# GateLoop and SwiGLU: one masked product per head and chunk, with complex gate products per 256 steps, in place of seven levels of products

## The chip, the cores and the metric

The kernel runs on one NeuronCore of a Trainium2 chip. The metric is the device time of one execution in microseconds (us). Engines are named as the profile names them: PE is TensorE (PEld its weight loads), DVE is VectorE, ACT is ScalarE, POOL is GpSimd, SP is SyncE, which here only issues DMAs. Everything is float32, except that three weight matrices arrive as float64.

## The reference, cut to what matters

Batch 4, 8 heads, 768 steps, 48 features in a head; then a SwiGLU feed-forward on 3072 tokens of width 384 with a hidden width of 1536.

```python
mag = np.sqrt(a_re * a_re + a_im * a_im)
scale = np.minimum(mag, 0.999) / (mag + 1e-06)
a_re_n, a_im_n = (a_re * scale, a_im * scale)
for t in range(S):
    new_re = ar * S_re - ai * S_im          # ar, ai: gates of step t, one per feature of k
    new_im = ar * S_im + ai * S_re
    kv = np.einsum('bhd,bhe->bhde', k[:, :, t], v[:, :, t])
    S_re, S_im = (new_re + kv, new_im)
    y[:, :, t] = np.einsum('bhd,bhde->bhe', q[:, :, t], S_re)
...
rms = np.sqrt(np.mean(x * x, axis=-1, keepdims=True) + 1e-06)
xn = x / rms * rms_g
g = xn @ w_gate
silu = g * (1.0 / (1.0 + np.exp(-g)))
val = xn @ w_val
return (silu * val @ w_out).astype(np.float32)
```

The gates of the test data have magnitudes from 0.850 to 1.045.

## The kernel before, in words

The work is cut into 24 chunks of 128 steps (six in each batch). The lines below are those of the profile.

**Gates** (`gates`, L89 to L162). For each batch and each of three slabs of 128 rows (head, feature) one pass over [128 x 768] turns the gates into a unit phasor and a magnitude (L103 to L126, with one `reciprocal` at L111), then multiplies up the phasors since the sequence's first step: a tree of complex products on strided views (`cmul`, L130, six instructions each; recorded at L98, where the helper `tt` stands). Cosine, sine and magnitude go to DRAM and come back by chunk with (head) on the free axis (L268 to L272).

**Levels** (`levels`, L278 to L337). Rotated q and k ([96 x 1024]: 96 rows of cosine and sine parts, 8 heads of 128 steps) meet in products for the diagonal (`s_diag`, L295), and then for each level m = 1, 2, 4, 8, 16 (`s_low`, L310, 64 instructions of 16 moving columns for a chunk and level) and m = 32, 64 (`s_high`, L322). After each level DVE masks the product into `dg` (L313) and multiplies half of q and half of k by the gates' products of the halves (L327, L328; recorded at L282), which the next level's products wait for. The result is the matrix of weights `amat`.

**Finish** (`finish`, L339 to L388). k is transposed (`kt_ps`, L350), the state's increment is a product with v (`state_ps`, L354), the output of a chunk has steps on the partitions (`y_ps`, L366 from `amat`, L368 from the state); it is normalised (L372 to L378, with a power on POOL at L376), transposed by PE (`xT_ps`, L385) and scaled (L386).

**Feed-forward** (`feed_forward`, L391 to L416) for groups of three chunks: `gate_ps` and `val_ps` (L400, [128 x 384], 36 products each), a sigmoid on ACT (L403), two products on DVE (L404, L405), then `out_ps` (L410) and the store (L415). A float32 product shows as two MATMUL instructions and two weight loads. **Weights** of 8 bytes are made float32 by DVE (`narrow`, L229 to L250), 18 pieces of [128 x 768], nine instructions each.

**Order.** The program is written out as one sequence: all gates of batch 0 come first (L418 to L425), then `step` (L431) turns between a chunk's levels, the finish of the chunk before, the gates of the next batch and, as a filler, the weights or the feed-forward. The order that runs on each engine is the framework's: a planner goes through the sequence with its own costs and gives each engine the earliest instruction of the sequence that its costs make ready, as far as buffers (the `bufs` of a tile's tag) are free. So the conversion of weights runs between the gates' instructions of batch 0, though it stands behind them in the sequence. On each engine and queue the resulting order is fixed: whoever waits holds up everything behind it. All DMAs are issued from the SP queue.

Of the kernel before, what the change touches and what calls it, by code (L numbers as in the profile page):

```python
# [12 lines left out]
"""  # L13
# [16 lines left out]
P = 128  # L30
C = 128          # steps in a chunk
BLK = 32         # steps in a diagonal block
# [3 lines left out]
SCALE = 2.0 ** 30    # gates are scaled by a power of two before they are squared  # L36
TINY = 2.0 ** -112   # squares of scaled gates below this: the gate's own value is 0 in float32
# [3 lines left out]
def gateloop_swiglu(  # L41
    ctx: ExitStack,
    tc: tile.TileContext,
    qT: bass.AP,      # [B * NCH, D, H * C]
    kT: bass.AP,      # [B * NCH, D, H * C]
    v: bass.AP,       # [B * S, H * D]
    a_re: bass.AP,    # [B, H * D, S]
    a_im: bass.AP,    # [B, H * D, S]
# [4 lines left out]
    out: bass.AP,     # [B * S, H * D]  # L53
# [7 lines left out]
    N = B * NCH  # L61
# [142 lines left out]
    def load_weights(stage):  # L204
# [299 lines left out]
```

## Time and profile before

| | us |
|---|---|
| median of 3 runs | 1413.6 |
| lowest, highest | 1412.28, 1414.24 |
| span of the profiled execution, first to last instruction | 1409.9 |
| first matmul starts at | 214.36 |
| PE, DVE, ACT busy in the span | 997.1, 1072.7, 225.6 |
| mean granted TensorE clock, share of 2.4 GHz | 0.896 |

The profiled execution is one of its own, and its span is the sum's measure; the median of the three timed runs lies 3.7 us above it, which is taken for what lies around the span. The page also cuts the span into 40 slices of 35 us: PE shows 0 in the first six, 4 to 9 tenths afterwards, and DVE 7 to 9 tenths up to slice 33.

### The profile page before, as it was taken

Reading aid. Unit: us, or ns where it says so; the run is one execution under the profiler, and the core shown is the slowest. Engines: PE = TensorE matmul, PEld = TensorE weight load, DVE = VectorE, ACT = ScalarE, POOL = GpSimd, SP = SyncE. Lnnn points to the kernel's source line nnn. Section 1 sums busy time; section 2 is a strip of 40 time slices with the busy share of each in tenths; the row PEclk is TensorE's granted clock in tenths of the full one; section 3 lists DMA queues with packets and bytes.
Section 4 is the critical chain, followed back from the end, with each engine's and each line's share of the span. In section 5 each row is a group of like instructions: output and inputs, shape, how many; then the busy total and the mean of one; then the engine's idle time right before and its main releaser. Section 6 shows DMA issues by size and latency. Waiting matters only on the chain.

```text
span 1409.9 us, 30973 instructions
## 1 busy us (share of the span) xinstructions
PE 997.1 (71%) x13352; PEld 702.6 (50%) x13352; DVE 1072.7 (76%) x2663; ACT 225.6 (16%) x453; POOL 34.1 (2%) x54
## 2 busy tenths in 40 slices
PE   0000005245399869986999699869997999799898
PEld 0000005235266555655665666556656667666555
DVE  7999998998988978897899798978955642543120
ACT  1000001111032211211222113112111211111110
POOL 2000000000100000000000000000000000000000
PEclk9999999999999958995899599958995997699899
DMA  6223242241022222302222313021213021100000
GB/s 173 69 99 106 84 119 63 74 136 45 24 75 62 85 62 53 97 29 52 74 57 85 82 39 96 31 73 30 63 63 80 24 52 40 30 1 7 12 1 17
DMA packets 63993, 86.94 MB, mean 62 GB/s; under 512 B 5488, under 2 KB 48496, under 8 KB 63856
## 3 DMA queue, kind: packets, MB, share of 16 engines
q1 hardware_dynamic: 63856, 84.96, 21.5%
q8 instruction: 105, 1.72, 0.5%
q14 instruction: 32, 0.26, 0.1%
HBM read 66.06 MB, written 18.87 MB: 60 GB/s over the span
## 4 chain that ended last, share of the span: by engine, by line
PE 51%; DVE 39%; issue 6%; ACT 1%; DMA 1%; POOL 1%; SPq 0%; POOLq 0%; DVEq 0%; ACTq 0%
PE gate_ps L400 13%; PE val_ps L400 11%; PE out_ps L410 6%; PE s_high L322 5%; DVE k L282 4%; PE s_low L310 4%; PE y_ps L366 4%; DVE w L98 3%; DVE cs L282 3%; PE state_ps L354 3%; PE y_ps L368 3%; DVE re L98 3%; DVE mg L111 2%; DVE s L98 2%; DVE m L98 2%
## 5 line engine op out<-in xcount | busy, mean ns | idle before, releaser
L400 PE MATMUL gate_ps<-xT,wg 128*128 128x384 f32 x576 | 231.7, 539 | 0.7 <-DVE xT L386 0.7
L400 PE MATMUL val_ps<-xT,wv 128*128 128x384 f32 x576 | 205.2, 492 | 0.0
L410 PE MATMUL out_ps<-wo,hT 128*128 128x384 f32 x576 | 192.0, 490 | 0.0
L295 PE MATMUL s_diag<-q,k 96*32 96x32 f32 x1536 | 23.4, 228 | 218.2 <-DVE k L282 214.4
L310 PE MATMUL s_low<-cs,k 96*32 96x16 f32 x7680 | 111.0, 199 | 86.0 <-DVE k L282 77.0
L310 PEld LDWEIGHTS s_low<-cs,k 96*32 96x32 f32 x7680 | 97.8, 131 | 131.2 <-issue 65.8
L400 PEld LDWEIGHTS val_ps<-xT,wv 128*128 128x128 f32 x576 | 110.9, 194 | 79.7 <-issue 5.7
L400 PEld LDWEIGHTS gate_ps<-xT,wg 128*128 128x128 f32 x576 | 113.1, 209 | 64.5 <-issue 13.8
L410 PEld LDWEIGHTS out_ps<-wo,hT 128*128 128x128 f32 x576 | 107.7, 190 | 71.3
L282 DVE TENSOR_TENSOR cs<-cs,bp 96x512 f32<-96x512 f32 x144 | 98.6, 685 | 49.9 <-PE s_high L322 49.7
L295 PEld LDWEIGHTS s_diag<-q,k 96*32 96x32 f32 x1536 | 20.4, 140 | 223.5 <-DVE k L282 214.4
L322 PE MATMUL s_high<-cs,k 96*32 96x32 f32 (+1 forms) x1152 | 79.2, 237 | 68.8 <-DVE k L282 47.4
L322 PEld LDWEIGHTS s_high<-cs,k 96*32 96x32 f32 (+1 forms) x1152 | 70.1, 150 | 88.7 <-issue 70.0
L404 DVE TENSOR_TENSOR sg<-gate_ps,sg 128x384 f32<-128x384 f32 x96 | 52.8, 550 | 63.7 <-ACT sg L403 63.4
L282 DVE TENSOR_TENSOR k<-k,bp 96x512 f32<-96x512 f32 x144 | 97.8, 679 | 0.0
L403 ACT ACTIVATE sg<-gate_ps 128x384 f32<-128x384 f32 x96 | 47.0, 489 | 276.2 <-PE gate_ps L400 263.0
L366 PE MATMUL y_ps<-v,amat 128*128 128x48 f32 x384 | 89.2, 334 | 0.7 <-ACT amat L324 0.7
L368 PE MATMUL y_ps<-state,cs 96*128 96x48 f32 x320 | 80.0, 340 | 0.0
L366 PEld LDWEIGHTS y_ps<-v,amat 128*128 128x128 f32 x384 | 75.2, 249 | 2.4 <-ACT amat L324 0.8
L405 DVE TENSOR_TENSOR hT<-val_ps,sg 128x384 f32<-128x384 f32 x96 | 53.1, 553 | 29.7 <-PE val_ps L400 29.6
L313 DVE COPY_PREDICATED dg<-pairs,s_low 128x128 f32<-128x128 int32 x120 | 41.3, 344 | 43.6 <-PE s_low L310 41.9
L368 PEld LDWEIGHTS y_ps<-state,cs 96*128 96x128 f32 x320 | 66.8, 258 | 0.0
(82 smaller groups left out, 1316.1 us busy)
## 6 DMA issues: line engine op xcount, KB each, us to landing
q<-in_q_dram SPq DMA_DIRECT2D x48, 192.0 KB, 3.4
k<-in_k_dram SPq DMA_DIRECT2D x48, 192.0 KB, 3.6
mg<-mag SPq DMA_DIRECT2D x48, 192.0 KB, 4.1
re<-in_a_re_dram SPq DMA_DIRECT2D x12, 384.0 KB, 3.2
im<-in_a_im_dram SPq DMA_DIRECT2D x12, 384.0 KB, 4.0
v<-in_v_dram SPq DMA_DIRECT2D x24, 192.0 KB, 2.6
raw<-in_w_gate_dram SPq DMA_DIRECT2D x6, 768.0 KB, 4.8
mag<-mg SPq DMA_DIRECT2D x12, 384.0 KB, 2.5
```

The source lines that it names most:

```text
L98: nc.vector.tensor_tensor(out=o, in0=x, in1=y, op=op)
L282: tt = lambda o, x, y: nc.vector.tensor_tensor(out=o, in0=x, in1=y, op=ALU.mult)
L295: nc.tensor.matmul(ps[bs, h], lhsT=k[:, h, bs], rhs=q[:, h, bs], start=True, stop=True)
L310: nc.tensor.matmul(ps[bs, h].rearrange("s (j r) -> s j r", r=m), lhsT=k[:, h, bs], rhs=rhs, start=True, stop=True)
L322: nc.tensor.matmul(ps[lo, h], lhsT=k[:, h, lo], rhs=qd[:, h, hi], start=True, stop=True)
L366: nc.tensor.matmul(ps[:, h], lhsT=am[:, h], rhs=vv[:, h], start=True, stop=prev is None)
L368: nc.tensor.matmul(ps[:, h], lhsT=qd[:, h], rhs=prev[:, h], start=False, stop=True)
L400: nc.tensor.matmul(p_, lhsT=w_[:, d, fs], rhs=xT[:, d], start=d == 0, stop=d == ND - 1)
L403: nc.scalar.activation(out=sg, in_=gp, func=AF.Sigmoid)
L404: nc.vector.tensor_tensor(out=sg, in0=gp, in1=sg, op=ALU.mult)
L405: nc.vector.tensor_tensor(out=hT[:, f], in0=vp, in1=sg, op=ALU.mult)
L410: nc.tensor.matmul(ps, lhsT=hT[:, f, i * C:(i + 1) * C], rhs=wo[:, f], start=f == 0, stop=f == NF - 1)
```

## The change

Features stay on the partitions and the work goes by 12 groups of 256 steps. Instead of unit phasors and levels it uses the complex products of the gates themselves since the group's first step, A, and the product R of the gates' inverse squared magnitudes: q is multiplied by A, and k by A times R, so that one product of q and k for a head and chunk, with a triangular mask, holds all weights (`chunk`). The state is turned by the group's whole product at a group's end (`turned`, through a small DRAM transpose and a swap of the halves by DMA). q and k are first copied DRAM to DRAM into row order (`rows_in`), multiplied with features on the partitions, written to DRAM and read back by chunk, for one group: 786 KB for each of `qd` and `kd` out, and four reads of 196 KB for each back. Reciprocal and square root are replaced by logarithm, exponential and a Newton step on ACT and DVE. y comes out with features on the partitions in slots of 64 rows, so that no transpose is needed before the feed-forward; the mean square over features is a product with ones (`rms`). The feed-forward takes 256 columns (two hidden tiles in one PSUM bank) and uses one Silu in place of a sigmoid and a product. Weights come by POOL's queue. At the end the ranges of R and of the sums are checked on the device; if they are exceeded, `step_by_step` (a loop over the steps, not shown) computes everything again.

```diff
--- before.py
+++ after.py
...
-    GC = 3               # chunks in a group of the feed-forward
+GC = 2
+T = GC * C
+L = 8
...
+    prep = work.enter_context(tc.tile_pool(name="prep", bufs=1))
+    unit = work.enter_context(tc.tile_pool(name="unit", bufs=2))
+    act = work.enter_context(tc.tile_pool(name="act", bufs=1))
+    ffn = work.enter_context(tc.tile_pool(name="ffn", bufs=2))
+    ps_f = work.enter_context(tc.tile_pool(name="ps_f", bufs=4, space=PSUM))
+    ps_s = work.enter_context(tc.tile_pool(name="ps_s", bufs=2, space=PSUM))
+    ps_m = work.enter_context(tc.tile_pool(name="ps_m", bufs=2, space=PSUM))
...
+    def sc_ln(o, x, **kw):
+        table = nc.scalar.preload_act_table_set("natural_log_exp_and_others")
+        behind(table, last_silu[0])
+        behind(sc(o, x, AF.Ln, **kw), table)
...
+        if slots:
+            for p0, r in slot_rows(ap[:, a:b]):
+                nc.gpsimd.dma_start(out=raw[p0:p0 + r.shape[0]], in_=r)
+        else:
+            nc.gpsimd.dma_start(out=raw, in_=ap.rearrange("(c p) f -> p c f", p=P)[:, c0:c1, a:b])
...
+        sc(tf, hi.bitcast(FP32), AF.Abs)
+        sc(hi.bitcast(FP32), hi.bitcast(FP32), AF.Sign)
+        ts(tf, tf, 1.125 * 2.0 ** -15, ALU.max)
+        ts(t, t, 3, ALU.logical_shift_left, 0x40000000, ALU.bitwise_xor)
+        ts(u, t, -2 ** 23, ALU.bitwise_and)
+        stt(uf, lo.bitcast(U32), 2.0 ** -52, uf, MUL, MUL)
+        tt(tf, tf, uf, ADD)
+        ts(t, t, 0x7FFFFFFF, ALU.bitwise_and)
+        tt(part, tf.rearrange("p (c f) -> p c f", f=cols), hi.bitcast(FP32).rearrange("p (c f) -> p c f", f=cols))
...
+    def norm(g):
+        u = G[g]
+        a3 = u["a3"] = prep.tile([P, L, 3, N], FP32, tag="a3", name="a3")
+        for i, x in ((1, "re"), (2, "im")):
+            nc.scalar.copy(out=blocked(a3[:, :, i]), in_=by_block(u[x]))
+        xa = prep.tile([P, 2, L, N], FP32, tag="xa", name="sq")
+        xb = prep.tile([P, 2, L, N], FP32, tag="xb", name="rs")
+        w, sq, rs, h = xa[:, 0], xa[:, 1], xb[:, 0], xb[:, 1]
+        sc(w, a3[:, :, 1], AF.Square)
+        sc(sq, a3[:, :, 2], AF.Square)
+        tt(w, w, sq, ADD)
+        sc_ln(h, w, bias=small)
+        sc(rs, h, AF.Exp, scale=-0.5)
+        sc(sq, rs, AF.Square)
+        tt(sq, sq, w)
+        sc(h, sq, AF.Identity, scale=-0.5, bias=c15, accum_out=guard[:, g:g + 1])
+        tt(rs, rs, h)
+        sc(h, rs, AF.Identity, scale=-EPS_MAG, bias=one)
+        ts(w, rs, CAP, MUL, 1.0, ALU.min)
+        tt(w, w, h)
+        a = a3[:, :, 1:3]
+        tt(a, a, w.unsqueeze(2).to_broadcast([P, L, 2, N]))
+        sc(a3[:, :, 0], a3[:, :, 2], AF.Copy, scale=-1.0)
+        sc(sq, rs, AF.Identity, scale=EPS_MAG, bias=one)
+        stt(sq, rs, 1.0 / CAP, sq, ALU.max, MUL)
+        r = h.rearrange("p i n -> p (i n)").rearrange("p (j t) -> p j t", j=ND)
+        sc(by_block(r), blocked(sq), AF.Square, accum_out=guard_sum[:, g:g + 1])
+        R = u["R"] = prep.tile([P, ND, T], FP32, tag="R", name="R")
+        for j in range(ND):
+            nc.vector.tensor_tensor_scan(out=R[:, j], data0=r[:, j], data1=r_max.to_broadcast([P, T]), initial=1.0,
+                                         op0=MUL, op1=ALU.min)
+        nc.scalar.copy(out=guard[:, NG * 2 + g * ND:NG * 2 + (g + 1) * ND], in_=R[:, :, T - 1])
...
+    def load_qk(g):
+        u = G[g]
+        for name, other in (("q", "re"), ("k", "im")):
+            pool, tag = (late[0], name) if late[0] else (prep, other)
+            u[name] = pool.tile([P, ND, T], FP32, tag=tag, name=name)
+            nc.sync.dma_start(out=u[name], in_=u[name, "rows"].rearrange("(j p) t -> p j t", p=P))
...
+    def products(g):
...
+        def cmul(x, y, m):
+            p, q = ta[:, 0, :, 0:m], tb[:, 0, :, 0:m]
+            tt(p, x[:, 1:2].to_broadcast([P, 2, m]), y[:, 1:3])
+            tt(q, x[:, 2:3].to_broadcast([P, 2, m]), y[:, 0:2])
+            tt(y[:, 1:3], p, q, ADD)
+        for i in range(1, L):
+            cmul(a3[:, i - 1], a3[:, i], N)
+        E = prep.tile([P, 3, N], FP32, tag="E", name="E")
+        nc.vector.tensor_copy(out=E[:, 1:3], in_=a3[:, L - 1, 1:3])
+        s = ND
+        while s < N:
+            ts(E[:, 0], E[:, 2], -1.0, MUL)
+            cmul(E[:, :, 0:N - s], E[:, :, s:N], N - s)
+            s *= 2
+        ts(E[:, 0], E[:, 2], -1.0, MUL)
+        m = N - ND
+        x, y = a3[:, 0:L - 1, :, ND:N], E[:, :, 0:m]
+        p, q = ta[:, :, :, 0:m], tb[:, :, :, 0:m]
+        shape = [P, L - 1, 2, m]
+        tt(p, x[:, :, 1:2].to_broadcast(shape), y[:, 1:3].unsqueeze(1).to_broadcast(shape))
+        tt(q, x[:, :, 2:3].to_broadcast(shape), y[:, 0:2].unsqueeze(1).to_broadcast(shape))
+        tt(x[:, :, 1:3], p, q, ADD)
+        nc.scalar.copy(out=a3[:, L - 1, 1:3], in_=E[:, 1:3])
+        A = prep.tile([P, 2, ND, T], FP32, tag="A", name="A")
+        for i in range(2):
+            nc.scalar.copy(out=by_block(A[:, i]), in_=blocked(a3[:, :, 1 + i]))
...
+        q, k, R = u["q"], u["k"], u["R"]
+        both = [P, 2, ND, T]
+        tt(k, k, R)
+        pool, tag = (late[0], "qa") if late[0] else (prep, "a3")
+        qa = pool.tile([P, 2, ND, T], FP32, tag=tag, name="qa")
+        tt(qa, A, q.unsqueeze(1).to_broadcast(both))
+        tt(A, A, k.unsqueeze(1).to_broadcast(both))
+        for name, t in (("kd", A), ("qd", qa)):
+            to = dram.tile([2, DM, T], FP32, tag=name, name=name + "_rows")
+            nc.sync.dma_start(out=to.rearrange("i (j p) t -> p i j t", p=P), in_=t)
+            for c in range(GC):
+                u[name, c] = unit.tile([D2, H, C], FP32, tag=name, name=name, bufs=3)
+                for i in range(2):
+                    nc.sync.dma_start(out=u[name, c][i * D:(i + 1) * D],
+                                      in_=to[i].rearrange("(h d) t -> d h t", d=D)[:, :, c * C:(c + 1) * C])
...
+    def chunk(g, c, state):
...
+        am = []
+        for a in range(2):
+            ps = ps_s.tile([C, hh, C], FP32, tag="s", name="s_ps")
+            for h in range(hh):
+                nc.tensor.matmul(ps[:, h], lhsT=k[:, a * hh + h], rhs=q[:, a * hh + h], start=True, stop=True)
+            t = unit.tile([C, hh, C], FP32, tag="am", name="am", bufs=3)
+            tt(t, ps, mask.unsqueeze(1).to_broadcast([C, hh, C]))
+            am.append(t)
...
+            ps = ps_m.tile([D2, H, D], FP32, tag="m", name="z_ps")
+            for h in range(H):
+                nc.tensor.matmul(ps[:, h], lhsT=kt[h // hh][:, h % hh], rhs=vv[:, h, 0:D], start=True, stop=True)
+            new = states[count[0] % 2]
+            count[0] += 1
+            if state is None:
+                nc.vector.tensor_copy(out=new[:, :, 0:D], in_=ps)
+            else:
+                tt(new[:, :, 0:D], state[:, :, 0:D], ps, ADD)
+        ps = ps_m.tile([P, NP, C], FP32, tag="m", name="y_ps")
+        for h in range(H):
+            to = ps[h % 2 * SLOT:(h % 2 + 1) * SLOT, h // 2]
+            nc.tensor.matmul(to, lhsT=vv[:, h], rhs=am[h // hh][:, h % hh], start=True, stop=state is None)
+            if state is not None:
+                nc.tensor.matmul(to, lhsT=state[:, h], rhs=q[:, h], start=False, stop=True)
+        x, s2 = u["x"], u["s2"]
+        cs = slice(c * C, (c + 1) * C)
+        sq = act.tile([P, NP, C], FP32, tag="ysq", name="ysq")
+        nc.scalar.copy(out=x[:, :, cs], in_=ps)
+        sc(sq, ps, AF.Square)
+        tt(sq[:, 0:2], sq[:, 0:2], sq[:, 2:4], ADD)
+        tt(s2[:, cs], sq[:, 0], sq[:, 1], ADD)
...
+        sc(w, ps, AF.Identity, scale=1.0 / DM, bias=eps)
+        sc_ln(h, w)
+        sc(rs, h, AF.Exp, scale=-0.5)
+        sc(h, rs, AF.Square)
+        tt(w, w, h)
+        sc(h, w, AF.Identity, scale=-0.5, bias=c15, accum_out=guard[:, NG + g:NG + g + 1])
+        tt(rs, rs, h)
+        for j in range(ND):
+            stt(x[:, j], x[:, j], gcol[:, j:j + 1], rs, MUL, MUL)
...
+    def hidden(g, f):
...
+        gp = ps_f.tile([P, FP, T], FP32, tag="f", name="gate_ps")
+        vp = ps_f.tile([P, FP, T], FP32, tag="f", name="val_ps")
+        for p_, w_ in ((gp, wg), (vp, wv)):
+            for i in range(FP):
+                fs = slice((f + i) * P, (f + i + 1) * P)
+                for d in range(ND):
+                    nc.tensor.matmul(p_[:, i], lhsT=w_[:, d, fs], rhs=x[:, d], start=d == 0, stop=d == ND - 1)
+        sg = ffn.tile([P, FP, T], FP32, tag="sg", name="sg")
+        last_silu[0] = sc(sg, gp, AF.Silu)
+        t = u["h", f] = ffn.tile([P, FP, T], FP32, tag="h", name="h", bufs=12)
+        tt(t, vp, sg)
...
+    load_gates(0)
+    rows_in(0)
+    load_qk(0)
+    norm(0)
+    products(0)
+    weights_in()
+    rows_in(1)
+    load_gates(1)
+    load_qk(1)
+    norm(1)
+    recurrence(0)
+    rms(0)
+    products(1)
+    rows_in(2)
+    load_gates(2)
+    load_qk(2)
+    norm(2)
+    recurrence(1)
+    rms(1)
+    for f in range(0, NF, FP):
+        weights_hidden(f)
+        for g in range(2):
+            hidden(g, f)
+    rows_in(3)
+    load_gates(3)
+    products(2)
+    for f in range(0, NF, FP):
+        weights(wo, w_out, False, f, f + FP, 0, DM)
+    early.close()
+    late[0] = work.enter_context(tc.tile_pool(name="late", bufs=1))
+    load_qk(3)
+    recurrence(2)
+    rms(2)
+    norm(3)
+    rows_in(4)
+    load_gates(4)
+    for g in range(2):
+        outputs(g)
+    products(3)
+    load_qk(4)
+    norm(4)
+    for g in range(2, NG):
+        if g + 3 < NG:
+            rows_in(g + 3)
+            load_gates(g + 3)
+        if g + 1 < NG:
+            recurrence(g + 1)
+        for f in range(0, NF, FP):
+            hidden(g, f)
+        if g + 2 < NG:
+            products(g + 2)
+        if g + 3 < NG:
+            load_qk(g + 3)
+        if g + 1 < NG:
+            rms(g + 1)
+        if g + 3 < NG:
+            norm(g + 3)
+        outputs(g)
+    work.close()
...
+    ts(ok[:, 0:NG], guard_sum, SUM_MAX, ALU.is_le)
+    ts(ok[:, NG:], guard, R_MAX, ALU.is_lt)
+    nc.vector.tensor_reduce(out=good, in_=ok, axis=mybir.AxisListType.X, op=ALU.min)
+    bad = fin.tile([1, 1], I32, name="bad")
+    with tc.tile_pool(name="ps_c", bufs=1, space=PSUM) as ps_c:
+        ps = ps_c.tile([1, 1], FP32, name="good_ps")
+        nc.tensor.matmul(ps, lhsT=good, rhs=one, start=True, stop=True)
+        ts(bad, ps, P - 0.5, ALU.is_lt)
+    taken = nc.values_load(bad[0:1, 0:1], min_val=0, max_val=1)
+    with tc.If(taken > 0):
+        step_by_step(tc, qT, kT, v, a_re, a_im, out, H, wg, wv, wo, gcol, ident)
...
```

## Rows read from the trace of the kernel before

**Rows 1.** The page's part 1, busy time of each engine over the span.
```profile
PE 997.1 (71%) x13352; PEld 702.6 (50%) x13352; DVE 1072.7 (76%) x2663; ACT 225.6 (16%) x453; POOL 34.1 (2%) x54
```
**Rows 2.** Busy time by stretch: length, busy per engine, granted clock, DMA share, GB/s.
```profile
0.00:211.00 211.00, 0.00 (x0) 0.00 (x0) 203.13 (x508) 12.36 (x14) 9.54 (x30) 1.00 0.37 108
...
500.00:700.00 200.00, 164.68 (x2353) 118.23 (x2353) 169.26 (x431) 40.80 (x80) 4.37 (x5) 0.77 0.23 61
...
1100.00:1200.00 100.00, 97.87 (x1240) 66.70 (x1238) 45.92 (x88) 15.84 (x36) 0.67 (x2) 0.92 0.14 36
```
**Rows 3.** Waits: who waited for whom, total us, times, longest.
```profile
PE s_diag L295 <- DVE k L282: 214.4, 1, 214.4
```
**Rows 4.** The page's part 4, engines' shares of the chain that ended last.
```profile
PE 51%; DVE 39%; issue 6%; ACT 1%; DMA 1%; POOL 1%; SPq 0%; POOLq 0%; DVEq 0%; ACTq 0%
```
**Rows 5.** Groups on VectorE by line: count | busy us, mean ns | idle before.
```profile
L282 DVE TENSOR_TENSOR cs<-cs,bp 96x512 f32<-96x512 f32 x144 | 98.6, 685 | 49.9 <-PE s_high L322 49.7
L282 DVE TENSOR_TENSOR k<-k,bp 96x512 f32<-96x512 f32 x144 | 97.8, 679 | 0.0
...
L111 DVE RECIPROCAL mg<-mg 128x768 f32<-128x768 f32 x12 | 59.3, 4943 | 0.0
L98 DVE TENSOR_TENSOR w<-im 128x192 f32<-128x192 f32 (+6 forms) x216 | 59.1, 274 | 0.0
...
L405 DVE TENSOR_TENSOR hT<-val_ps,sg 128x384 f32<-128x384 f32 x96 | 53.1, 553 | 29.7 <-PE val_ps L400 29.6
...
L282 DVE TENSOR_TENSOR k<-k,cs 96x1024 f32<-96x1024 f32 x24 | 29.1, 1213 | 0.3 <-issue 0.3
```
**Rows 6.** Timeline of VectorE in the first stage: start us, us, instruction.
```profile
21.94 0.95 DVE L98 TENSOR_TENSOR w<-w,r 128x768 f32<-128x768 f32 x1
22.81 0.55 DVE L238 TENSOR_SCALAR u<-raw 128x768 int32<-128x768 int32 x1
23.28 0.55 DVE L118 TENSOR_SCALAR w<-w 128x768 f32<-128x768 f32 x1
...
32.59 0.48 DVE L98 TENSOR_TENSOR s<-re 128x192 f32<-128x192 f32 x1
32.98 0.49 DVE L98 TENSOR_TENSOR w<-im 128x192 f32<-128x192 f32 x1
```
**Rows 7.** Timeline of TensorE around two chunks' ends: start us, us, instruction.
```profile
962.05 0.39 PE L366 MATMUL y_ps<-v,amat 128*128 128x48 f32 x2
962.27 0.39 PE L368 MATMUL y_ps<-state,cs 96*128 96x48 f32 x2
...
969.21 0.74 PE L310 MATMUL s_low<-cs,k 96*32 96x16 f32 x64
...
970.26 2.10 PE L400 MATMUL gate_ps<-xT,wg 128*128 128x384 f32 x6
...
1269.95 0.88 PE L350 MATMUL kt_ps<-ident,k 96*128 96x96 f32 x8
...
1271.12 1.56 PE L354 MATMUL state_ps<-v,kt 128*96 128x48 f32 x16
...
1281.48 4.17 PE L400 MATMUL gate_ps<-xT,wg 128*128 128x384 f32 x6
```
**Rows 8.** The chain that ended last in order of time: its last piece.
```profile
1382.96 23.23 PE out_ps L410 x72
```
**Rows 9.** Groups on ScalarE by line: count | busy us, mean ns | idle before.
```profile
L403 ACT ACTIVATE sg<-gate_ps 128x384 f32<-128x384 f32 x96 | 47.0, 489 | 276.2 <-PE gate_ps L400 263.0 <-DVE hT L405 4.5 <-DVE im L98 4.2
...
L108 ACT ACT_TABLE_LOAD x8 | 10.3, 1283 | 4.7 <-DVE w L98 4.5
...
L103 ACT ACTIVATE s<-re 128x768 f32<-128x768 f32 x12 | 10.1, 842 | 210.4 <-DVE re L98 208.7 <-DMA re<-in_a_re_dram 1.6
```
**Rows 10.** DMA issues: count, KB each, median us from issue to landing.
```profile
raw<-in_w_gate_dram SPq DMA_DIRECT2D x6, 768.0 KB, 4.8
...
cs<-cos SPq DMA_DIRECT2D x24, 192.0 KB, 3.7
```
**Rows 11.** Timeline of the SyncE queue late in the kernel: start us, us.
```profile
1163.89 17.59 SPq L415 DMA_DIRECT2D out_dram<-ot  x3
```

More of the change, by code (lines that the diff above doesn't have):

```diff
@@ new lines, in gateloop_swiglu @@
+    small = const("small", [P, 1], 2.0 ** -30)
+    r_max = const("r_max", [P, 1], R_MAX)
+    ones = const("ones", [P, P], 1.0)
+    ident = const("ident", [P, P])
+    make_identity(nc, ident)
+    mask = const("mask", [C, C], 1.0)
+    nc.gpsimd.affine_select(out=mask, in_=mask, pattern=[[1, C]], compare_op=ALU.is_ge, fill=0.0,
+                            base=0, channel_multiplier=-1)
+    v_pad = [const(f"v{i}", [C, H, SLOT], 0.0) for i in range(2)]
+    states = [const(f"state{i}", [D2, H, SLOT], 0.0) for i in range(2)]
@@ new lines, in turned @@
+    def turned(g, state):
+        u = G[g]
+        swap = unit.tile([D2, H, D], FP32, tag="swap", name="swap")
+        for i in range(2):
+            nc.sync.dma_start(out=swap[i * D:(i + 1) * D], in_=state[(1 - i) * D:(2 - i) * D, :, 0:D])
+        new = states[count[0] % 2]
+        count[0] += 1
+        turn = u["turn"].unsqueeze(3)
+        tt(swap, swap, turn[:, 1].to_broadcast([D2, H, D]))
+        tt(new[:, :, 0:D], state[:, :, 0:D], turn[:, 0].to_broadcast([D2, H, D]))
+        tt(new[:, :, 0:D], new[:, :, 0:D], swap, ADD)
+        return new
@@ new lines, in rms @@
+    def rms(g):
+        u = G[g]
+        x = u["x"]
+        ps = ps_m.tile([P, T], FP32, tag="m", name="ss_ps")
+        nc.tensor.matmul(ps, lhsT=ones, rhs=u["s2"], start=True, stop=True)
+        w, rs, h = (act.tile([P, T], FP32, tag=n, name=n) for n in ("rw", "rr", "rh"))
+        sc(w, ps, AF.Identity, scale=1.0 / DM, bias=eps)
[5 more added lines that the diff above has]
+        tt(rs, rs, h)
+        for j in range(ND):
+            stt(x[:, j], x[:, j], gcol[:, j:j + 1], rs, MUL, MUL)
@@ new lines, in outputs @@
+    def outputs(g):
+        u = G[g]
+        for c in range(GC):
+            ps = ps_f.tile([C, DM], FP32, tag="f", name="out_ps")
+            for f in range(NF):
+                nc.tensor.matmul(ps, lhsT=u["h", f // FP * FP][:, f % FP, c * C:(c + 1) * C], rhs=wo[:, f],
+                                 start=f == 0, stop=f == NF - 1)
+            ot = ffn.tile([C, DM], FP32, tag="ot", name="ot")
+            nc.scalar.copy(out=ot, in_=ps)
+            n = g * GC + c
+            nc.sync.dma_start(out=out[n * C:(n + 1) * C, :], in_=ot)
@@ L419, in gateloop_swiglu @@
-    loaded = first
-    for j in range(ND):
-        t, loaded = loaded, None
-        if j + 1 < ND:
-            loaded = load_gates(0, j + 1)
-        for _ in gates(0, j, t):
-            pass
-    load_unit(0)
-    stack = ctx.enter_context(ExitStack())
-    filler = load_weights(stack.enter_context(tc.tile_pool(name="stage", bufs=2)))
-    ffn = None
-    def step(*generators):
-        running = list(generators)
-        while running:
-            for x in list(running):
-                if next(x, running) is running:
-                    running.remove(x)
-            next(filler, None)
@@ L463, in gateloop_swiglu @@
-    for _ in filler:
-        pass
+                    nc.tensor.matmul(p_, lhsT=w_[:, d, f * P:(f + 1) * P], rhs=xT[:, d], start=d == 0, stop=d == ND - 1)
+            sg = pool.tile([P, C], FP32, tag="fsg", name="fsg", bufs=2)
+            nc.scalar.activation(out=sg, in_=gp, func=AF.Silu)
+            tt(h[:, f], vp, sg)
+        ps = psum.tile([C, DM], FP32, tag="p3", name="fo_ps")
+        for f in range(NF):
+            nc.tensor.matmul(ps, lhsT=h[:, f], rhs=wo[:, f], start=f == 0, stop=f == NF - 1)
```

562 lines of the change are left out of this document (261 added, 301 removed).

## The prediction

> **What bounds the kernel now.** I read the page's busy times first, then the same by stretch, the waits, the chain, and the groups and timelines for prices. Over the span no engine is full: VectorE (DVE) is busy for 76%, TensorE (PE) for 71% [rows 1]. By stretch there are two regimes. For the first 211 us DVE works without a gap (203 us) and PE not at all [rows 2]: the first matmul waits 214.4 us for the rotated k of chunk 0 [rows 3], behind all gates of batch 0 and most weight conversions. Afterwards both are near full and take turns: PE's levels wait for DVE's factors, DVE's masks for PE's products. In 500 to 700 us PE is busy 82% at a mean granted clock of 0.77, DVE 85%. Only late, with no gates left, PE is the bound: 97.9% busy in 1100 to 1200 us, DVE 46% [rows 2]. The chain that ended last is 51% PE and 39% DVE [rows 4]. So DVE's work is what has to shrink first, and under it lies a PE bound.
>
> **DVE after the change.** Prices first. A DVE instruction on float32 costs 0.95 us for 768 elements and 1.21 us for 1024 [rows 5, 6], so 1.04 ns for each element and about 0.15 us fixed; the next one starts some 0.08 us before the end (0.95 us lasts, 0.87 us passes to the next start), and a tensor_scalar of 768 takes 0.46 us of pace [rows 6]. I use pace: 0.07 us + 1.04 ns for each element. The 192-element products of before cost 0.48 us [rows 6], on strided views; the new ones lie side by side, so I take 0.27.
> - norm, one group: five of 768 (4.4), one tensor_scalar (0.5), one of 1536 (1.7), three scans of 256. No row has a scan: between 0.34 us (an ordinary two-input instruction) and double; I take 0.5. Sum 8.1.
> - products: 21 of 192 elements (5.7), the copy of E (0.2), five doublings with 15 of some 155 elements (3.5) and six small (0.8), three of 1302 (4.3), one of 768 (0.9), two of 1536 (3.3). Sum 18.7.
> - two chunks: each two masks of 512 from PSUM (0.6 each, by the 0.55 us of 384 in [rows 5]), the state (0.5), two sums (0.5): 4.4 together. The turn 1.4 in eight of twelve groups, rms 1.7, six products of the hidden layer 3.6.
> Sum 37.4 to 38 us for a group, 456 for twelve. Weights: seven instructions instead of nine, 18 x (4 x 0.46 + 3 x 0.87) = 82 us. Together 538 us, half of 1072.7 [rows 1]. The levels, the reciprocal (59.3 us) and all strided products [rows 5] are gone.
>
> **PE after the change**, at the higher of its two clock levels (2.4 GHz). 72 output products take 23.23 us [rows 8], 323 ns for 384 columns, so 0.84 ns a column and 215 ns for 256. A group's hidden layer is 144 instructions: 31.0 us; its outputs 48 x 0.323 = 15.5. The weight loads stay covered: a load of 128 columns passes in 0.11 us, as the y_ps pairs show (0.22 us for two) [rows 7]. A chunk: 16 score instructions of 128 columns at 0.11 (1.8), transposes 0.88, the state's increment 1.56 [rows 7], 32 y instructions with 64 weight columns and 128 moving columns, 0.107 each by the column price: 3.4. Sum 7.65. Twelve groups: 12 x 46.5 + 24 x 7.65 + 5 for the sums of squares = 747 us. The transposes before the feed-forward are gone.
>
> For y two 64-column halves of the array are addressed in turn. The 64 s_low instructions go to four column quarters and take 0.74 us [rows 7]; one after the other, their 64 x 16 columns at 0.84 ns would be 0.86 us even with every weight load hidden, so some ran beside each other. The Trainium skill (TensorEngine Tiling (Array Packing), Key Properties) says that different tiles load weights and multiply in parallel; by it y would take half, 1.7 us a chunk, and the kernel 41 us less. I keep 3.4, since here up to four instructions of one half stand in a row; half of it, 1.7, is the lower bound, and loads not hidden at all (64 columns, half of the 0.11 us above) give the upper, 5.2.
>
> **The first stage.** What must pass before the steady state: the gates of groups 0 to 2, all weights, recurrence 0 and 1 with their hidden layers. On DVE: 82 + 3 x 26.8 + 3 x (4.4 + 1.4) + 2 x 1.7 + 12 x 0.6 = 190 us. DVE is the bound here as it was before, since the weights can fill its gaps: the same planner does so now. To this come some 9 us until the first operands have passed ACT (two 384 KB loads, then copies and squares at 0.84 us each [rows 9]) and 15 us of gaps in the chain: norm's steps alternate between ACT and DVE, a group's gates wait for q, k and the store of the group before (one buffer each), and the trip through DRAM takes about 9 us (768 KB land in 4.8, 192 KB in 3.7 us [rows 10]). End: 215 us. PE starts far earlier, at about 60 us (4 for the load, 17 for norm, 25 for products with their copies, 10 for DRAM and issue), and by 215 us has done six chunks and two hidden layers, 46 + 62 = 108 us of its 747.
>
> **The steady state.** 639 us of PE are left, and in each of the ten remaining periods 62 us of PE stand against 38 of DVE and about 24 of ACT (14 instructions of 768 elements at 0.84 us, 14 of about 512 at 0.6 by the sigmoid's 0.49 for 384 [rows 9], a few small ones). ACT's two table changes a group (for norm and rms, and back to Silu) are four loads of 1.28 us [rows 9], 61 us in all, and lie beside PE: rms of the next group passes under the 15.5 us of outputs. The Trainium skill (ScalarE: Activation LUTs, What ACT_TABLE_LOAD costs) speaks against such alternation: each change costs the load and a drain, together 2.7 us, an estimated 128 us of ACT here; no row shows the drain, and ACT would still be less than half full. DMA: the small pieces make it busier than before (up to half busy by the prices of its packets), but everything is asked for a period ahead. So I take PE as the bound with the stretch of the one stage where it was the bound before: 97.9% busy at a mean clock of 0.92 [rows 2], a factor 1 / (0.979 x 0.92) = 1.11. 639 x 1.11 = 709 us.
>
> **Sum.** 215 + 709 + 10 for the end (last store, the ranges' test, the branch; no row shows one: 2 to 20) = 934 us of span against 1409.9. The median of the runs lies 3.7 us above that span, so 938, and I say **940 us**.
>
> **The rivals.**
> 1. *The group's chain sets the period, not PE.* norm of group g+3 waits for the last Silu of group g, then norm (18), products with copies (21) and DRAM (9) follow on single buffers, 48 us alone, with every step queued behind masks and hidden products on DVE and ACT. If those queues, or the SP queue, where a waiting store holds up what stands behind it (17.6 us for three stores [rows 11]) and some 35 issues a group now pass, stretch the period from 69 to 85 us: 215 + 19 + 850 + 14 = 1098. For it: every order is fixed by a planner's costs. Against: 20 us of slack.
> 2. *The first stage overlaps better and the halves run at once.* PE 747 - 41, stretch 1.03: 215 + 598 x 1.03 + 14, about 845. For it: s_low's row. Against: clock losses in every stage but the dense ones [rows 2].
> 3. *Slower: PE stays at 1.2 GHz.* The same six gate products take 2.10 us or 4.17 us [rows 7], and the clock is lowest where PE is busy with small products and gaps. If the new short products (y, scores, between waits for masks) held PE at the lower level throughout, the rest would cost 639 x 2 x 1.05 and the kernel 1570. It decides from about 80% of the work at 1.2 GHz on: (1414 - 229) / 639 = 1.85. Against: 47 of a period's 62 us are feed-forward, and where that was dense the clock was 0.92 [rows 2].
> 4. *The change doesn't do what it says:* the test at the end fails and the loop over 768 steps runs, with over ten DVE instructions of 576 elements (0.75 us by the price above) a step: more than 5 ms. The largest product of inverse squares over 256 steps of these data is 2^79, against 2^124 allowed, and the largest sum 949 against 4096.
>
> **How the numbers follow.** Forecast 0.63, rival 1 0.20, rival 2 0.13, rival 3 0.02, rival 4 0.01, and 0.01 for no change. A difference of 0.2%, 3 us, is about what a measurement can tell. Faster 0.96, same 0.01, slower 0.03. The forecast's own range is 880 to 1010 (stretch 1.05 to 1.2, first stage 200 to 235, y 1.7 to 5.2 us a chunk); reaching into rivals 1 and 2 it becomes 860 to 1080.
>
> **What would show it.** Right: the first matmul near 60 us, DVE without gaps until about 215 and some 540 us busy in all, PE over 90% busy afterwards, a period of about 69 us, hidden instructions at 215 ns. Wrong: PE idle once in each period, waiting for qd or kd (rival 1) or for x; a mean clock under 0.8 after 215 us (rival 3); hidden instructions far above 215 ns; a first stage over 250 us, with DVE waiting for ACT or for weights.

## The result, and the profile after

The changed kernel takes 919.4 us, median of four runs (918.5 to 923.5), against 1413.1 us: a ratio of 0.651 (95% interval 0.6496 to 0.6529). Forecast were 940 us. The ratios of the experiments below are to the kernel before, too, which took 1412.3 to 1413.6 us beside them. The span of the profiled execution fell from 1409.9 to 917.9 us.

The page of the changed kernel, its busy times and its chain's shares [rows 1, 4]:

```profile
PE 726.5 (79%) x3898; PEld 590.7 (64%) x3898; DVE 564.6 (62%) x1110; ACT 379.6 (41%) x555; POOL 34.9 (4%) x74
...
PE 50%; DVE 20%; DMA 13%; ACT 10%; issue 3%; SPq 2%; DVEq 0%; ACTq 0%
```

DVE lost 508 us and PE 271. Where before DVE and PE were on the chain with 39% and 51%, transfers now hold 13% of it. Busy time by stretch (stretch and length, then PE, PEld, DVE, ACT, POOL, granted clock, DMA share, GB/s), which answers [rows 2]:

```profile
0.00:215.00 215.00, 50.19 (x301) 44.68 (x302) 139.59 (x253) 90.47 (x121) 31.63 (x70) 0.82 0.72 155
215.00:400.00 185.00, 169.77 (x871) 136.96 (x873) 142.43 (x285) 85.42 (x123) 3.25 (x4) 0.94 0.46 111
400.00:900.00 500.00, 498.63 (x2707) 404.82 (x2703) 282.40 (x573) 202.79 (x311) 0.00 (x0) 1.00 0.35 77
```

Three regimes: a first stage in which nothing is full, a transition, and 500 us in which PE is busy for 99.7% at the full clock. PE's idle time is 917.9 - 726.5 = 191.4 us: 164.8 before 215 us, some 16.6 from there to its last output at 907.7, 10 after it. So what is left to win from PE's idle time lies almost wholly in the first stage. PE's timeline there (start, duration, instruction, in brackets how long PE was idle before and what ended it), against the one wait of [rows 3]:

```profile
79.93 3.75 PE L361 MATMUL s_ps<-qd,kd 96*128 96x128 f32 x16 [79.93 <-DMA kd<-kd_rows]
...
117.35 4.34 PE L458 MATMUL gate_ps<-x,wg 128*128 128x256 f32 x12 [10.29 <-issue]
...
173.37 3.75 PE L361 MATMUL s_ps<-qd,kd 96*128 96x128 f32 x16 [49.09 <-DMA kd<-kd_rows]
...
214.85 5.07 PE L458 MATMUL gate_ps<-x,wg 128*128 128x256 f32 x12 [12.56 <-ACT raw L117]
...
337.58 3.76 PE L361 MATMUL s_ps<-qd,kd 96*128 96x128 f32 x16 [9.93 <-DMA kd<-kd_rows]
...
391.69 3.78 PE L361 MATMUL s_ps<-qd,kd 96*128 96x128 f32 x16 [5.30 <-DMA kd<-kd_rows]
```

The scores of groups 0, 1, 3 and 4 wait for `kd`, the trip of k through DRAM (those of group 2, at 274 us, don't). PE's dense work begins at 214.85 us, where the forecast had it (215), but not for its reason. Before `kd` stands this on the chain of the first recurrence, and again on that of the second:

```profile
52.58 12.15 DMA flat<-end
...
67.68 8.19 DMA kd_rows<-A
76.23 3.57 DMA kd<-kd_rows
...
145.95 12.11 DMA flat<-end
...
161.18 8.24 DMA kd_rows<-A
```

`flat` is the small transpose that turns the state: 4.5 KB. The SP queue's timeline shows why k waits for it:

```profile
52.58 0.39 SPq L319 DMA_DIRECT2D flat<-end  x1
54.03 0.38 SPq L335 DMA_DIRECT2D qd_rows<-qa  x1
64.74 2.84 SPq L324 DMA_DIRECT2D turn<-flat  x4
67.68 0.92 SPq L335 DMA_DIRECT2D kd_rows<-A  x1
```

SP issues in order. The reads of `turn` wait until `flat` has landed, 12.15 us after its issue, and the store of k, whose product DVE had finished by 56.5 us, stands behind them until 67.68.

### The profile page after: what moved, and what is told of

Same layout as the page of the kernel before. It is cut to its first block, busy times and chain, and to the rows that moved or that the text cites. A ratio compares the mean times of both kernels' runs of the same rounds, so it can differ in the third digit from the quotient of the medians.

```text
span 917.9 us, 10670 instructions
## 1 busy us (share of the span) xinstructions
PE 726.5 (79%) x3898; PEld 590.7 (64%) x3898; DVE 564.6 (62%) x1110; ACT 379.6 (41%) x555; POOL 34.9 (4%) x74
## 4 chain that ended last, share of the span: by engine, by line
PE 50%; DVE 20%; DMA 13%; ACT 10%; issue 3%; SPq 2%; DVEq 0%; ACTq 0%
PE gate_ps L458 16%; PE val_ps L458 15%; DMA flat<-end 7%; PE out_ps L469 5%; PE s_ps L361 4%; DMA kd_rows<-A 4%; PE z_ps L377 3%; ACT rs L117 3%; DVE tb L107 3%; PE y_ps L387 3%; DVE ta L107 3%; DVE a L107 3%; PE y_ps L389 2%; DVE R L258 2%; DMA kd<-kd_rows 2%
## 5 line engine op out<-in xcount | busy, mean ns | idle before, releaser
L458 PE MATMUL gate_ps<-x,wg 128*128 128x256 f32 x864 | 204.7, 386 | 22.9 <-ACT raw L117 12.6
L458 PE MATMUL val_ps<-x,wv 128*128 128x256 f32 x864 | 198.3, 379 | 0.0
L458 PEld LDWEIGHTS gate_ps<-x,wg 128*128 128x128 f32 x864 | 165.7, 194 | 48.5 <-ACT raw L117 13.3
L469 PE MATMUL out_ps<-wo,h 128*128 128x384 f32 x576 | 188.1, 486 | 0.0
L458 PEld LDWEIGHTS val_ps<-x,wv 128*128 128x128 f32 x864 | 164.1, 190 | 22.4 <-issue 0.2
L361 PE MATMUL s_ps<-qd,kd 96*128 96x128 f32 x384 | 59.0, 312 | 145.6 <-DMA kd<-kd_rows 144.2
L469 PEld LDWEIGHTS out_ps<-wo,h 128*128 128x128 f32 x576 | 109.3, 190 | 73.8 <-issue 0.3
L361 PEld LDWEIGHTS s_ps<-qd,kd 96*128 96x128 f32 x384 | 54.4, 221 | 151.8 <-issue 92.1
L107 DVE TENSOR_TENSOR h<-val_ps,sg 128x512 f32<-128x512 f32 x72 | 49.5, 688 | 144.3 <-PE val_ps L458 143.2
L107 DVE TENSOR_TENSOR a<-ta,tb 128x192 f32<-128x192 f32 x96 | 48.0, 500 | 2.1
L117 ACT ACTIVATE wt<-raw 128x768 f32<-128x768 f32 x18 | 16.3, 904 | 68.2 <-DMA raw<-in_w_gate_dram 56.5
## 6 DMA issues: line engine op xcount, KB each, us to landing
qd_rows<-qa SPq DMA_DIRECT2D x12, 768.0 KB, 13.3
```

What stands on the lines that cost most here:

```text
L107: return nc.vector.tensor_tensor(out=o, in0=x, in1=y, op=op)
L117: return nc.scalar.activation(out=o, in_=x, func=func, **kw)
L361: nc.tensor.matmul(ps[:, h], lhsT=k[:, a * hh + h], rhs=q[:, a * hh + h], start=True, stop=True)
L458: nc.tensor.matmul(p_[:, i], lhsT=w_[:, d, fs], rhs=x[:, d], start=d == 0, stop=d == ND - 1)
L469: nc.tensor.matmul(ps, lhsT=u["h", f // FP * FP][:, f % FP, c * C:(c + 1) * C], rhs=wo[:, f], start=f == 0, stop=f == NF - 1)
```

## The experiments

Two theories of the first stage stood against each other: the forecast's (DVE's work bounds it), and one from the trace of after (a chain of ACT, DVE, transfers and one SP queue bounds it, with `flat` as its dearest link). All diffs are against the changed kernel.

**Without the conversion of the weights.** Six of seven DVE instructions of each of 18 pieces go. ACT's two passes stay, in the other order, and so do the DMAs, of which SP issues a few of the row copies and loads in another order.

```diff
+        sc(hi.bitcast(FP32), hi.bitcast(FP32), AF.Sign)
         sc(tf, hi.bitcast(FP32), AF.Abs)
-        sc(hi.bitcast(FP32), hi.bitcast(FP32), AF.Sign)
-        ts(tf, tf, 1.125 * 2.0 ** -15, ALU.max)
-        ts(t, t, 3, ALU.logical_shift_left, 0x40000000, ALU.bitwise_xor)
-
-        ts(u, t, -2 ** 23, ALU.bitwise_and)
-        stt(uf, lo.bitcast(U32), 2.0 ** -52, uf, MUL, MUL)
-        tt(tf, tf, uf, ADD)
-        ts(t, t, 0x7FFFFFFF, ALU.bitwise_and)
```

> Edit: of the seven DVE instructions that make a piece of the weights float32 only the last is left, so the weights' values are wrong; loads and ACT's two passes stay. That takes 18 x (4 x 0.46 + 2 x 0.87) = 64 us off DVE, all before about 300 us. Rival D (DVE sets the first stage): about 64 us less, near 855. Theory Q (a chain of DMAs sets it, DVE idles a third of it): under 12 us less, 907 to 919.

Measured: 905.2 us (899.2 to 907.1), ratio 0.6415 [0.6396, 0.6434]. 62 us less of DVE bring 14 us, where a bound would have given back nearly all of it. That DVE bounds the first stage is refuted. The dense part starts 18 us earlier in the profile, which is of the fastest of the four runs:

```profile
196.59 5.24 PE L451 MATMUL gate_ps<-x,wg 128*128 128x256 f32 x12 [14.49 <-issue]
```

DVE's instructions are links of a chain, and some left with the conversion: of the 195 longest pieces of the chain before 215 us DVE's are 39 us here and 50 in the changed kernel. What SP's changed order adds or takes is not known.

**`flat` behind k and q.** The same DMAs, issued after the stores and reads of `kd` and `qd`.

```diff
-            flat = dram.tile([3, DM], FP32, tag="flat", name="flat")
-            nc.sync.dma_start(out=flat.rearrange("k (j p) -> p k j", p=P), in_=end)
...
+        if (g + 1) % NGB:
+            flat = dram.tile([3, DM], FP32, tag="flat", name="flat")
+            behind(nc.sync.dma_start(out=flat.rearrange("k (j p) -> p k j", p=P), in_=end), last)
```

> Edit: the small DMAs of the group's turn (flat out, turn back) go behind the stores and reads of kd and qd on the SP queue. Theory Q (the first stage is a chain of DMAs, and SP's fixed order holds kd's store behind the 12 us of flat): some 11 us less on each of the three trips that lie on the path (group 0 at 52.6 us, group 1 at 146, group 3 at 313), first matmul near 69 us instead of 79.9, total about 885 us. Rival D (the prediction's: DVE's work sets the first stage): DVE has the same work, PE's dense part still begins at about 215 us, total 919 within 4.

Measured: 909.8 us (908.0 to 910.6), ratio 0.6441 [0.6424, 0.6457]: 10 us, not the 34 expected. The first scores start at 69.50 us, ten earlier, the second at 159.27. The chain shows where the rest went:

```profile
67.86 18.32 DMA re<-in_a_re_dram
...
157.65 19.96 DMA im<-in_a_im_dram
```

The next group's gates are now what comes behind `flat` on the queue, and a load of 384 KB takes 18 to 20 us instead of the median 6.2 to 6.9 of the changed kernel. ACT's next instruction in order waits for the second of them until 177.6 us and copies `kt` for PE only after it, which costs PE 10.05 us at 170 us. The price went to the next in line: this speaks for the transfer itself being dear, and not only its place, which the next run tests.

**`flat` in rows.** PE transposes the [128 x 9] tile, so that nine rows of 512 bytes go out in place of 1152 pieces of 4 bytes.

```diff
-            nc.sync.dma_start(out=flat.rearrange("k (j p) -> p k j", p=P), in_=end)
+            ps = ps_m.tile([3 * ND, P], FP32, tag="m", name="end_ps")
+            nc.tensor.transpose(ps, end.rearrange("p k j -> p (k j)"), ident)
+            lines = prep.tile([3 * ND, P], FP32, tag="lines", name="lines")
+            nc.scalar.copy(out=lines, in_=ps)
+            nc.sync.dma_start(out=flat.rearrange("k (j p) -> (k j) p", p=P), in_=lines)
```

> Edit: the group's whole product is transposed by PE first, so that flat goes out as 9 rows of 512 bytes instead of 1152 pieces of 4 bytes; SP's order stays. Theory S (the small pieces themselves hold up everything behind them on the queue, as the load of re took 18 us behind flat when flat was moved): flat lands in about 2.5 us instead of 12, some 10 us less on each of the trips of groups 0, 1 and 3, 885 to 895 us. Rival O (only SP's order cost, which the first run already gave back): about 910, as that run.

Measured: 900.9 us (898.4 to 902.0), ratio 0.6368 [0.6357, 0.6378], 18.5 us below the changed kernel: well below the rival's 910, but not as low as Theory S had it. Its SP queue:

```profile
53.24 0.35 SPq L323 DMA_DIRECT2D flat<-lines  x1
53.88 0.40 SPq L339 DMA_DIRECT2D qd_rows<-qa  x1
54.49 2.71 SPq L328 DMA_DIRECT2D turn<-flat  x4
57.30 0.42 SPq L339 DMA_DIRECT2D kd_rows<-A  x1
```

k's store is issued 10.4 us earlier. The store of q, which stands right behind `flat` on the queue, lands in 5.1 us (median of twelve) where it took 13.3. The scores start at 71.03 and 155.93 us, the dense part at 198.69 instead of 214.85, and the waits of 9.93 and 5.30 us for `kd` at 327 and 386 us are gone. PE idles 27 us less (164.2 instead of 191.4), but is busy 10 us longer (736.1 instead of 726.5), 3 of them for the eight transposes. This is the largest single cost found.

**The hidden layer group by group.** PE's order was hidden(0, f), hidden(1, f) in turn, so that group 0's hidden layer stopped after one pair of tiles until group 1 was there.

```diff
     for f in range(0, NF, FP):
         weights_hidden(f)
-        for g in range(2):
-            hidden(g, f)
+        hidden(0, f)
+    for f in range(0, NF, FP):
+        hidden(1, f)
```

> Edit: while the weights arrive, the hidden layer of group 0 goes through all its tiles before that of group 1, instead of the two in turns. Theory B (after the first tile PE's fixed order makes group 0's hidden layer wait for group 1's rms at 214 us, while five of the six weight tiles are ready by 155 us): PE does four more tiles, 21 us, in its idle time before 173 us, 895 to 902. Rival W (the weights come too late): within 5 us of 919.

Measured: 913.3 us (907.7 to 918.1), ratio 0.6448 [0.6425, 0.6471]: 6 us less, between the two expectations. PE does what was meant: 77.5 us busy by 215 us instead of 50.2. But the profile, which is of the slowest of the four runs, has a span only 1.6 us shorter (916.3 us):

```profile
0.00:215.00 215.00, 77.50 (x432) 66.35 (x433) 147.55 (x271) 94.94 (x127) 31.72 (x70) 0.85 0.72 155
215.00:400.00 185.00, 163.42 (x818) 129.69 (x817) 133.14 (x258) 90.95 (x125) 2.89 (x4) 0.91 0.45 111
400.00:850.00 450.00, 442.42 (x2430) 360.35 (x2430) 280.17 (x576) 193.51 (x297) 0.00 (x0) 0.98 0.39 85
```

Of the 27 us that PE works more before 215 us, 13 come back as idle time after it (39.7 us instead of 26.6), and 13 as a longer busy time in all (739.1 us instead of 726.5, at a mean granted clock of 0.933 instead of 0.943). PE waits for `kd` as before (7.80 us at 320 us, 7.56 at 383) and, 2 us, for the weights of the output. The filler was early; the chain of the groups' recurrences was not.

**Both.** Rows for `flat` and the hidden layer group by group.

```diff
+            nc.tensor.transpose(ps, end.rearrange("p k j -> p (k j)"), ident)
...
+        hidden(0, f)
+    for f in range(0, NF, FP):
+        hidden(1, f)
```

> Edit: both of the two above (flat by rows, hidden layers in turn). If the two idle stretches are separate, their gains add: 919 - 28 - 20, about 870. If they are the same idle time, about 890.

Measured: 891.8 us (889.5 to 892.9), ratio 0.6308 [0.6296, 0.6320]. That is 27.6 us below the changed kernel, where the two alone gave 18.5 and 6: a little more than their sum. The number is that of the second expectation, but by luck: the gains do add, and both had been taken too high. It is the fastest version found, 3% below the changed kernel. Of its span of 889.4 us PE is idle for 155, 124 of them still before 215 us:

```profile
0.00:215.00 215.00, 91.21 (x470) 77.89 (x471) 155.36 (x288) 97.55 (x133) 33.16 (x71) 0.85 0.69 158
```

**The gates' loads on another queue**, ACT's, on top of both, to take them from behind q and k on SP.

```diff
-            nc.sync.dma_start(out=u[name], in_=ap[b].rearrange("(j p) s -> p j s", p=P)
+            nc.scalar.dma_start(out=u[name], in_=ap[b].rearrange("(j p) s -> p j s", p=P)
```

> Edit: as the run before, and the gates' loads are issued from ACT's queue, so that they don't stand behind SP's reads of qd. Theory: norm of group 1 starts when q and k of group 0 are done with, at about 60 us instead of 78, and the second recurrence up to 15 us earlier: 855 to 870. Rival: ACT waits with the load at the head of its queue and gives the gain back, or PE has its remaining work filled by then: within 5 us of the run before.

Measured: 901.1 us (899.7 to 909.3), ratio 0.639 [0.6357, 0.6423]: 9 us worse than without it, against both expectations. The second scores do start earlier, at 150.34 instead of 161.15 us, but the first later, at 78.73 instead of 71.09: on their chain the store of k lands in 8.32 us instead of 4.18. And the gates now come before the weights' conversion on DVE, and PE waits for that:

```profile
PE gate_ps L462 <- DVE wg L107: 23.8, 3, 10.7
PE val_ps L462 <- DVE wv L107: 13.6, 3, 12.2
```

(Waits: us in total, times, longest; 4.2 and 0.7 us in total without this edit.) Here the weights' conversion holds PE up on its own account. How the 9 us divide between the two isn't shown.

**y's halves one after the other.** Even heads first, then odd ones: the same 704 y instructions, in another order.

```diff
-        for h in range(H):
+        for h in [*range(0, H, 2), *range(1, H, 2)]:
```

> Edit: y's products go through the even heads and then the odd ones, so that neighbours on PE share one half of the array's columns instead of taking turns. Theory H (the two halves run side by side, which is why four y instructions pass in 0.22 us instead of 0.43): y of a chunk goes from 1.8 to about 3.5 us, 24 x 1.7 = 41 us more PE, of which all but the first two groups' is on the path: 945 to 960. Rival (an instruction of 64 columns is simply half as long): no change, 919 within 3.

Measured: 945.7 us (944.2 to 953.0), ratio 0.6715 [0.6683, 0.6746], 26 us slower; PE is busy for 752.2 us instead of 726.5, so all of PE's added work shows in the time. PE's timeline of the changed kernel, where each y line holds four instructions of two heads:

```profile
279.20 0.44 PE L387 MATMUL y_ps<-am,v 128*64 128x128 f32 x4
279.42 0.44 PE L389 MATMUL y_ps<-qd,state 96*64 96x128 f32 x4
279.64 0.44 PE L387 MATMUL y_ps<-am,v 128*64 128x128 f32 x4
```

and of this one, with the change of halves at 281.46:

```profile
280.58 0.38 PE L387 MATMUL y_ps<-am,v 128*64 128x128 f32 x2
280.80 0.38 PE L389 MATMUL y_ps<-qd,state 96*64 96x128 f32 x2
281.02 0.38 PE L387 MATMUL y_ps<-am,v 128*64 128x128 f32 x2
281.24 0.38 PE L389 MATMUL y_ps<-qd,state 96*64 96x128 f32 x2
281.46 0.44 PE L387 MATMUL y_ps<-am,v 128*64 128x128 f32 x4
```

A line passes in 0.22 us in both; it holds four instructions there and two here. So two neighbours of different halves run side by side, at a pace of 55 ns for each instruction of 128 columns, and 110 where they share a half. This is what the Trainium skill's "TensorEngine Tiling (Array Packing)", Key Properties, says of different tiles, and the measurement agrees.

**More DVE work.** Twelve more products of 768 elements, read by nobody, in each `norm` from group 5 on.

```diff
+        if g >= 5:
+            junk = prep.tile([P, N * L], FP32, tag="junk", name="junk")
+            for _ in range(12):
+                tt(junk, wg[:, 0, 0:N * L], wv[:, 0, 0:N * L])
```

> Edit: twelve more DVE products of 768 elements in norm of groups 5 to 11, 10.4 us each, that nobody reads: 73 us more of DVE in the steady part. Theory P (PE alone sets the period of about 58 us, DVE has over 15 us spare in each): 919 to 925. Rival 1 of the prediction (the group's chain through DVE sets the period): 10 us more in each of seven periods, about 990.

Measured: 957.9 us (954.1 to 961.7), ratio 0.679 [0.6760, 0.6821]: 39 us more, and both expectations miss. The edit did not do what it was meant to: the products wait for nothing but weights, so the order drew all 84 of them ahead of 402 us, 17 us of them between 119 and 190 us and 62 into the stretch from 262 to 405, where the changed kernel's PE still waits for `kd`. Those waits grew, and went on for 200 us after the last extra product (column 1 is the start, the bracket the idle time before):

```profile
364.72 1.51 PE L375 MATMUL kt_ps<-ident,kd 96*128 96x96 f32 x8 [10.98 <-DMA kd<-kd_rows]
...
437.04 1.51 PE L375 MATMUL kt_ps<-ident,kd 96*128 96x96 f32 x8 [9.78 <-DMA kd<-kd_rows]
...
547.04 3.78 PE L365 MATMUL s_ps<-qd,kd 96*128 96x128 f32 x16 [7.32 <-DMA kd<-kd_rows]
...
601.29 3.75 PE L365 MATMUL s_ps<-qd,kd 96*128 96x128 f32 x16 [3.82 <-DMA kd<-kd_rows]
```

The four are 32 us, where the changed kernel's two are 15. In all PE idles 26 us more than there (217.5 instead of 191.4) and is busy 9 us longer (735.8 instead of 726.5). The granted clock was 0.93 in 400 to 500 us, where it is 1.00 without the edit; from 700 us on PE is at 99.6% again. So more DVE work in the steady part, the test that was meant, was not made.

What the run does show is a pace of the chain. Where two recurrences in turn wait for it, they start 54 us apart: 547.04 and 601.29 here, 337.58 and 391.69 in the changed kernel (53.8 without the conversion, 55.3 with the halves apart, but 62.3 with the hidden layer group by group). PE's own period is 58 us, so a late chain catches up about 4 us a period (7.32 to 3.82; 9.93 to 5.30). That PE bounds the steady state by no more than that is argued from these pairs, not shown: the chain passes through PE itself (from 547 to 566 us here), and the pairs' intervals differ.

## Why the prediction was right, and where not

The forecast was 2% high and its own case came true: PE bounds the kernel, at a high clock, and 26 us more of PE's work, in the run with the halves apart, were 26 us more of time. Against the sum 215 + 709 + 10 = 934 us of span stand 215 + 693 + 10 = 918. (The other 5 us of the difference lie around the span, 1.5 us where 3.7 were taken, and in rounding up.) That two of the terms agree hides three errors in the middle one.

**The step "DVE is the bound here" failed.** The first stage lasts 215 us as forecast, but DVE is busy for 140 of them, not 190, and taking away its conversion brings 14 us. In the place of the bound is a chain through all engines: its 195 longest pieces in this stretch are 51 us of DMA, 50 of DVE, 49 of ACT and 34 of PE. The forecast had 9 us for the trip through DRAM; it took 27 in group 0 (52.6 to 79.9 us), 12 of them for `flat`, a transfer that the sum did not price at all. Rival 1 named the mechanism, a waiting DMA at the head of SP's queue, but put it into the steady state. So the 215 came out right by luck.

**The step "has done six chunks and two hidden layers, 108 us, by 215 us" failed.** Done were four chunks, the first pair of hidden tiles and two sums of squares, 4 x 5.8 + 5.2 + 0.9 = 29 us at the full clock (50 us busy in fact, at a mean granted clock of 0.82). The first matmul came at 79.93, not 60, and PE's fixed order held group 0's hidden layer behind group 1's recurrence. 79 us more were left.

**PE's total was 53 us too high.** y takes 55 ns for an instruction, not 107: 40 us less. I had weighed the trace's own hint (the quarters of s_low [rows 7]) and kept the higher price; the lower bound was right. The reason for it, four instructions of one half in a row, does not hold: the loop still writes them so, and those of the other half ran beside them. Another 13 us: four of the 24 chunks, a batch's last, compute no state, and the four first read none. 747 - 53 = 694.

**The stretch of 1.11 was too high.** 665 us were left (694 - 29) and took 693, a factor of 1.04. I carried over 97.9% and a clock of 0.92 from a stretch in which levels lay between the feed-forward [rows 2]; PE now is at 99.7% and 1.00 for 500 us. Rival 2's 1.03 was nearer. (In the page's slices of before DVE is at 7 to 9 tenths up to slice 29, about 1020 us, and not 33 as said under the table there, and PE at 2 to 9 tenths after its start; with [rows 2] that makes the end of the kernel a stage of its own.) Together: 26 us more work left (79 - 53), at a stretch 0.07 lower, which takes back 45.

**What held.** Hidden instructions take 216 ns (2.59 us for twelve; forecast 215), outputs 15.5 us a group, as these pieces of the chain show, the last of which answers [rows 8]:

```profile
222.51 2.59 PE gate_ps L458 x12
...
788.53 15.48 PE out_ps L469 x48
...
892.22 15.49 PE out_ps L469 x48
```

The end took the 10 us. The period is 58 us (recurrences at 456.1, 513.5, 572.0 and 631.4 us), which is PE's work in it with y at half price (46.5 + 2 x 5.9 + 0.4), not 69. Rivals 3 and 4 did not come.

**Rival 1's slack was nearer to 4 us than to 20**, as far as the pairs above tell. The chain's interval is 54 to 55 us in four of the five pairs, not the 48 that I added up, and PE's is 58, not 69. Up to 392 us the chain did hold PE up, and 39 us were lost when DVE was loaded more before 402 us. The forecast's main case may have been nearer to its rival than its chances of 0.63 and 0.20 say.

**DVE's and ACT's terms** were low, without visible consequence. DVE: 564.6 against 538 (in which the weights' 82 should have been 80). The price of 0.27 us for 192 elements holds where the next instruction does not need the result, but not where it does, as DVE's timeline of the first group shows:

```profile
32.89 0.36 DVE L107 TENSOR_TENSOR ta<-a 128x192 f32<-128x192 f32 x1
33.16 0.35 DVE L107 TENSOR_TENSOR tb<-a 128x192 f32<-128x192 f32 x1
33.55 0.36 DVE L107 TENSOR_TENSOR a<-ta,tb 128x192 f32<-128x192 f32 x1
33.94 0.36 DVE L107 TENSOR_TENSOR ta<-a 128x192 f32<-128x192 f32 x1
```

Three pass in 1.05 us (32.89 to 33.94), where 0.81 were taken. Other prices that differ, on DVE and ACT (count, then busy us and mean ns, then idle before):

```profile
L258 DVE TENSOR_TENSOR_SCAN R<-rs,r_max 128x256 f32<-128x256 f32 x36 | 22.3, 674 | 2.3 <-ACT rs L117 1.4
```

```profile
L312 ACT COPY A<-a 128x768 f32<-128x768 f32 x24 | 36.0, 1548 | 26.1 <-DVE a L107 22.3 <-issue 3.9
...
L117 ACT ACTIVATE sq<-a 128x768 f32<-128x768 f32 x24 | 19.7, 848 | 0.1
```

A scan of 256 lasted 0.67 us, and three in a row 1.86 (taken 0.5 of pace, bounds 0.34 and 0.68). ACT's copies between the order of steps and that by blocks took 1.55 us (taken: 0.84); these stand on the chain of every group, and `A<-a` alone is 3.0 us before each store.

ACT's table loads are 31, not 48, since rms of one group and norm of another share a change; they take 1283 ns each as before [rows 9]. One of them in ACT's timeline:

```profile
205.80 0.92 ACT L117 ACTIVATE sq<-rs,one 128x768 f32<-128x768 f32 x1
206.73 1.28 ACT L117 ACT_TABLE_LOAD   x1
208.03 0.42 ACT L117 ACTIVATE rr<-rh 128x256 f32<-128x256 f32 x1
```

From the end of one activation to the start of the next the change took 1.31 us. No row shows the drain of about 1.4 us that the Trainium skill's "ScalarE: Activation LUTs", What ACT_TABLE_LOAD costs, adds to every switch; here the measurement decides.

**Not tried:** separate buffers for the first groups' q and k, another place in the order for the output's weights, fewer row copies ahead of them. What bounds the 124 us that PE still idles in the best version's first 215 us is narrowed to the chain from gates to `kd` and to the weights' conversion, but not divided between the two.

## What to carry to other kernels

A start-up stage in which no engine is full is a chain: price it link by link, DMAs and the queue's order included, and not by the busy time of its fullest engine. Ask of every small transfer how many pieces it has and what is issued behind it; 4.5 KB cost more here than 768 KB. And work brought forward pays in full only if what comes next is ready earlier too: the hidden layer's new order was worth 6 us alone and 9 once the chain behind it was shorter.

## What the runs showed of the hardware that was not expected

- 1152 pieces of 4 bytes took 12 us to land, and what followed on the same queue was slow too: 18 to 20 us for a load of 384 KB and 13.3 for a store of 768 KB, which took 5.1 behind nine rows of 512 bytes.
- Two 64-column products on neighbouring halves run at once, at a pace of 55 ns for each instruction instead of 110, if the order changes the half from head to head.
- ACT's copy of 768 float32 values takes 1.55 us where it reorders them; a square of as many that runs on takes 0.85.
- A change of ACT's table took 1.31 us, from the end of one activation to the start of the next, in which the load's 1.28 us leave no room for more.
- With PE busy for over 99% the granted clock was 1.00 for 500 us; with waits of 4 to 10 us between 400 and 600 us it was 0.93 to 0.95 in the run with more DVE work.
